# Attention and a capped mixture of experts on one core: where the gate's logits stand among the attention units, how fast the routing list is worked off, and three idle products

## The chip, the core and the metric

The kernel runs on one core of a Trainium2 chip. It is a single launch, written with a hand-made order for every engine. Times are device microseconds of one execution, as the median of several; a difference is given as time after over time before.

The engines are named as in the profile: PE is TensorE's matmul side and PEld its loading of weights (the stationary operand), which overlaps PE; DVE is VectorE, ACT ScalarE, POOL GpSimd, and SP the engine that issues most DMAs. "SPq" in a row is SP's sequencer.

## The reference

Two steps. Attention over 4 batches x 8 heads x 768 positions x 64, with a mask that leaves each position the first 8 positions and the 96 last ones up to itself, and a linear bias by distance. Then a mixture of experts on the 3072 tokens of width 512: each token goes to the expert with the greatest gate logit, and of an expert's tokens only the 80 with the greatest gate value are computed.

```python
scores = scale * np.matmul(q, k.transpose(0, 1, 3, 2)) + bias
scores = np.where(is_global | is_local, scores, -1e9)
a = np.exp(scores - np.max(scores, axis=-1, keepdims=True))
a = a / (np.sum(a, axis=-1, keepdims=True) + 1e-09)
x = np.matmul(a, v)                       # then to (3072, 512)

logits = x @ w_gate                       # 512 x 8
expert_idx = np.argmax(logits, axis=1)
gate_w = probs[np.arange(N), expert_idx]  # softmax of the logits
for e in range(8):
    tok_idx = np.where(expert_idx == e)[0]
    # if there are more than 80: keep those with the 80 greatest gate_w
    h = np.maximum(x[tok_idx] @ w1[e], 0.0)        # 512 -> 1024
    out[tok_idx] = gate_w[tok_idx, None] * (h @ w2[e])
```

All other rows of the output are zero.

## The kernel before

**Stages.** Constants and warming up, then the attention stage, then a search for each expert's threshold and the choice of its tokens, then the experts. All the loads of an SP queue (queries `q`, keys `kt`, values `va` and `vb`, expert weights `w`) and the stores of zeros and of x go through one queue in the order written down. Expert weights are loaded from early in the attention stage on.

**Units.** The 3072 tokens are 24 tiles of 128. A unit u is half a tile: tile t = u // 2, four of its eight heads (g = u % 2). The loop over units issues, for unit u and on PE in this order: the score products (L181) of u; inside them the transposes (L242, L250) of the probabilities of u - 2; and `weigh(u - 3)`, the products with the values (L289 for the local window, L298 for the part before it). On DVE stand four operations (L201) that add the bias and find the maximum of a unit, the sum's reciprocal (L213, L214), and half of the copies `ta` of the transposes (L265); on ACT four exponentials (L205) and the other half of the copies (L259); on POOL the scaling of the probabilities (L222).

**The buffer `pair`.** Both head groups of a tile are summed up in one PSUM buffer, `pair`. When its second half is done (in an even unit: u - 3 is odd), ACT copies it to `ut` (L312, `A.copy(out=uts[t]...)`). The next tile's first product L289 stands in the unit after, an odd one, and overwrites `pair`, so it waits for this copy. `ut` is a buffer for two tiles, so that it is full after every fourth unit.

**Logits.** For two tiles t and t + 1 together, four products L318 (one for each pair of heads; `logits1`) put the logits, 32 rows a pair, in the buffer `lps`. DVE copies them to `ls` (L322), two transposes L330 (`logits2`) bring `ls` back with a token in each partition, and DVE adds up the four parts for each tile (L359, in `collect`). In the loop before the change they stood by the unit's number modulo 4:

```python
if u % 4 == 1 and 9 <= u:
    logits2((u - 9) // 2, 2)      # ahead of weigh(u - 3)
...
if u % 4 == 0 and 8 <= u:
    logits1((u - 8) // 2, 2)      # directly ahead of weigh(u - 3)
```

**Routing.** The tiles form groups of 6, 6, 6, 4 and 2. When the last logits of a group are there, generators are put at the end of a list `routing`: softmax pieces (L500 to L511), compares of every token's value with 127 candidate thresholds (`choose`, L545), a count (six products L601 for a group of six, one a tile), and the columns of later one-hot products (`columns`, L581 to L588, on POOL). `routes(n)` at the end of a unit runs n steps of that list. Before the change n was 2, 3 in units with u % 4 = 3, and 5 from unit 41 on. The generator `rest` does the compares, then yields twice without an instruction, then counts.

**After the last unit** the order comes from the string DRAIN. Between the search and the experts ten products (L594, `busy`) with no use of their result keep PE running, then the experts begin: `prepare` splits a quarter of an expert's first weights into two rounded parts (L813 on ACT, L817 on DVE), three more idle products L953 use these parts (STAY), and `tokens(0)` transposes the gathered rows of the first expert (L835, copied at L836), which the first expert's products L843 take. The rows come by an indirect DMA from x; SP waits for the same rows before a small transfer (L947).

Of the kernel before, what the change touches and what calls it, by code (L numbers as in the profile page):

```python
# [22 lines left out]
P = 128  # L23
NB = S // P
NT = B * NB
# [13 lines left out]
QUARTERS = [(k, e, c) for k, e in LAYERS for c in range(4)]  # L39
NHI, NLO = (4, 1), 6  # L40
GROUPS = (6, 6, 6, 4, 2)
# [10 lines left out]
HELD, EVERY, AHEAD, LATE = 2, 3, 14, 2  # L52
FROM, INSIDE = 18, 14
HOLD = 20


DRAIN = (
# [4 lines left out]
ROWS = (3, 1, 3, 1, 0, 0, 0)  # L62
WAKE, FILL = 7, ((0, 2), (1, 4), (2, 4), (3, 1), (4, 1))
WARM = (0, 0, 0, 0, 0, 0, 2, 10)
STAY = (3, 0)
SPLIT = (4, 4, 4)
FAR = 1.0e6
END = object()
# [3 lines left out]
def fast_path(tc, a, out, cst, x_dram, inp):  # L72
    nc = tc.nc
    V, A, G, T = nc.vector, nc.scalar, nc.gpsimd, nc.tensor
    ident = cst["ident"]

    with ExitStack() as ctx:
# [6 lines left out]
        lps = psl.tile([P, 512], F32, name="lps")  # L84
# [56 lines left out]
        with tc.tile_pool(name="at_sb", bufs=2) as sp, ExitStack() as sctx:  # L141
# [13 lines left out]
            def begin(u):  # L155
                st[u] = [
                    sp.tile([P, 4], F32, tag="nm", bufs=3, name=f"nm{u}"), sp.tile([P, 4], F32, tag="z", bufs=3, name=f"z{u}"),
                    sp.tile([P, 4, WH], F32, tag="ts", name=f"ts{u}"), pwz[u % 3][:, :4 * WH].rearrange("p (j k) -> p j k", j=4),
                ]
# [156 lines left out]
            def logits1(t, n):  # L316
                for pr in range(NP):
                    T.matmul(  # L318
                        lps[32 * pr:32 * pr + 32, :n * P], cst["wgn"][:, pr, :], st[t, "ut"][:, pr, :n, :], start=True, stop=True,
                        skip_group_check=True)  # L320
                ls = sp.tile([P, n * P], F32, tag=f"ls{n}", name=f"ls{t}")
                (A.copy if t == NT - 2 else V.tensor_copy)(out=ls, in_=lps[:, :n * P])  # L322
                st[t, "l"] = ls

            def logits2(t, n):

                ls = st.pop((t, "l"))
                if n == 2:
                    for i in range(2):
                        T.transpose(out=part(t + i), in_=ls[:, P * i:P * i + P], identity=ident)  # L330
                else:
                    T.matmul(lgs(t), ls, cst["pick"], start=True, stop=True, skip_group_check=True)
                for i in range(n):
                    collect(t + i)

            def part(t):
                return lps[:, :P] if t % 2 else lps[:, 2 * P:3 * P]

            def lgs(t):
                if t == NT - 1:  # L340

                    if t not in st:
                        st[t] = psa.tile([P, 512], F32, tag="tp0", name="lgl")[:, :E]
                    return st[t]
                if t not in st:
                    st[t] = psa.tile([P, 512], F32, tag="tp1", name="lgk")[:, :E]
                return st[t]
# [28 lines left out]
            def routes(n):  # L376
                for _ in range(n):
                    while routing and next(routing[0], END) is END:
                        routing.pop(0)

            routing, cst["later"], cst["landed"] = [], [], []
            nu = 2 * NT
            late = late_constants(nc, a, cst)
            keys = inp.keys(3)
# [6 lines left out]
            for u in range(nu - 1):  # L391
                if u == 0:
                    for _ in cst["first"]:
                        pass
                begin(u)
                scores(u)
                if u % 4 == 1 and 9 <= u:
                    logits2((u - 9) // 2, 2)
                if 2 <= u:
                    copied(u - 2)  # L400
                if u == 1:
                    for _ in window:
                        pass
                    for z in pwz:
                        G.memset(z[:, 4 * WH:], 0.0)
                    G.memset(cst["zero"], 0.0)
                if u > 2:
                    for _ in range(3):
                        next(late, None)
                if u % 4 == 0 and 8 <= u:  # L410
                    logits1((u - 8) // 2, 2)
                if 3 <= u:
                    idle(2 if u == 3 else 0)
                    weigh(u - 3)
                if u % 2 == 0 and 3 <= u // 2 + 2 < NT:
                    inp.load_q(u // 2 + 2, hold=u < HOLD)
                    for _ in range(1 + (u == 20)):
                        next(keys, None)
                if u % 2:
                    if 2 <= u // 2 + 1 < NT:  # L420
                        inp.load_v(u // 2 + 1, hold=u < HOLD)
                    for k in ASKS[u // 2]:
                        next(dict(w=ahead, o=wipe).get(k, iter(())), None)
                routes(5 if u > 40 else 2 + (u % 4 == 3))
            u = nu - 1
            begin(u)
            scores(u)
# [39 lines left out]
        early = [hip.tile([P, DF], F32R, tag="hi", name=f"early{i}") for i in range(3)]  # L467
# [7 lines left out]
class Route:  # L475
# [52 lines left out]

    def rest(self, cn, capm):
        yield from self.choose()  # L530
        yield
        yield
        count(self.nc, cn, [self])
        if capm is not None:
            yield
            yield self.nc.vector.tensor_tensor(out=capm[:P - 1], in0=capm[:P - 1], in1=cn[:P - 1], op=ALU.subtract)
        yield from self.finish()
# [245 lines left out]
def experts(tc, out, cst, x_dram, inp, raw, weights, lps, early, hip, wipe):  # L783
    nc = tc.nc
    V, A, G, T = nc.vector, nc.scalar, nc.gpsimd, nc.tensor
# [3 lines left out]
    with tc.tile_pool(name="ffn", bufs=2) as fp, tc.tile_pool(name="hl", bufs=NLO) as hl, \  # L789
# [141 lines left out]
        fill, ready, held = iter(QUARTERS), {}, []  # L931
# [9 lines left out]
        with tc.manual_schedule(engines=ORDERED | {ET.SP}):  # L941
            targets(nc, cst)
            for e in range(E):
                gather(e)
                if e == 0:
                    prepare(1, True)
            nc.sync.dma_start(out=cst["scl"][:1], in_=xgs[0][:1, :2])  # L947
            for _ in islice(weights, NW - AHEAD - LATE):
                pass
            for n in range(2):  # L950
                prepare(n)
                for _ in range(STAY[n]):
                    T.matmul(lps[:, :480], early[0][:, :P], ready[QUARTERS[n]][1][:, :480], start=True, stop=True, skip_group_check=True)  # L953
            tokens(0)
            prepare(2)
            for e in range(E - 1):
                def amid(c):
                    if e == 1 and c == 2:
                        hidden(0)
                    if c == (4 if e else 2):  # L960
                        tokens(e + 1)

                layer1(e, amid)
                amid(4)
                if e:
                    layer2(e - 1, lambda c: c == 2 and hidden(e))
                    finish(e - 1)
            layer2(E - 2)
            finish(E - 2)
            last(E - 1)  # L970
            layer2(E - 1, lambda c: c == 1 and hidden(E - 1, (1,)))
            finish(E - 1)
# [487 lines left out]
```

## Time and profile before

| | |
|---|---|
| median of 3 runs | 259.3 us (257.15 to 259.46) |
| the profiled execution | 259.51 us, with a span of 257.7 us |
| busy in the span | PE 239.6 us (93%), PEld 169.2 (66%), DVE 213.7 (83%), ACT 208.0 (81%), POOL 107.5 (42%) |
| mean granted clock of PE | 0.977 |

The span is the time from the first to the last instruction; the rest of the measured time lies around it. Shares over the span mix stages, so the rows below are cut by stretches. A row of a window gives the stretch and its length, then each engine's busy time with its number of instructions (x), the granted clock of PE as a share of full speed, the share of time that the 16 DMA engines were busy, and what they moved. A row of the timeline gives start and duration, engine, line and operation, what it wrote from what with partitions x elements, how many instructions it stands for, and in square brackets how long the engine idled before it and who released it. All rows are of one execution. Matmuls are pipelined and their ends are modelled.

### The profile page before, as it was taken

Reading aid. Unit: us, or ns where it says so; the run is one execution under the profiler, and the core shown is the slowest. Engines: PE = TensorE matmul, PEld = TensorE weight load, DVE = VectorE, ACT = ScalarE, POOL = GpSimd, SP = SyncE. Lnnn points to the kernel's source line nnn. Section 1 sums busy time; section 2 is a strip of 40 time slices with the busy share of each in tenths; the row PEclk is TensorE's granted clock in tenths of the full one; section 3 lists DMA queues with packets and bytes.
Section 4 is the critical chain, followed back from the end, with each engine's and each line's share of the span. In section 5 each row is a group of like instructions: output and inputs, shape, how many; then the busy total and the mean of one; then the engine's idle time right before and its main releaser. Section 6 shows DMA issues by size and latency. Waiting matters only on the chain.

```text
span 257.7 us, 9711 instructions
## 1 busy us (share of the span) xinstructions
PE 239.6 (93%) x3587; PEld 169.2 (66%) x3587; DVE 213.7 (83%) x782; ACT 208.0 (81%) x584; POOL 107.5 (42%) x214
## 2 busy tenths in 40 slices
PE   7989998998899999999998798999999999999991
PEld 2567766766677777877667655666666666666660
DVE  3777778987779799898987778999999898999860
ACT  3889899998899999999886636887979898979740
POOL 7667674644445745457470638810000022221111
PEclk9999999999999999999999659999999999999998
DMA  5758999999998999988649976999999999999101
GB/s 145 235 159 218 330 287 280 282 304 300 274 301 247 287 284 316 319 251 230 216 138 311 384 265 204 347 333 401 404 410 408 407 397 398 389 405 364 51 25 36
DMA packets 49086, 73.06 MB, mean 284 GB/s; under 512 B 3688, under 2 KB 23528, under 8 KB 49032
## 3 DMA queue, kind: packets, MB, share of 16 engines
q1 hardware_dynamic: 47864, 69.74, 81.3%
q0 software_dynamic: 1024, 2.62, 3.2%
q8 instruction: 30, 0.49, 0.8%
q14 instruction: 24, 0.20, 0.3%
q10 hardware_dynamic: 144, 0.00, 0.0%
HBM read 58.46 MB, written 13.89 MB: 281 GB/s over the span
## 4 chain that ended last, share of the span: by engine, by line
PE 63%; ACT 13%; DVE 10%; DMA 4%; issue 4%; POOL 3%; SPq 0%; POOLq 0%; DVEq 0%; ACTq 0%
PE hp L843 17%; PE yp L843 17%; ACT pwz L205 9%; PE ring L181 6%; PE pair L289 5%; PE pair L298 3%; DMA kt<-in_kT_dram 3%; PE tp L242 3%; ACT ta L259 2%; DVE ts L201 2%; POOL pwz L222 2%; PE tp L898 2%; PE lps L318 1%; DMA q<-in_q_dram 1%; PE lps L330 1%
## 5 line engine op out<-in xcount | busy, mean ns | idle before, releaser
L205 ACT ACTIVATE pwz<-ts,nm 128x168 f32<-128x168 f32 (+1 forms) x192 | 81.5, 427 | 10.3 <-DVE z L213 6.0
L222 POOL TENSOR_TENSOR pwz<-pwz,z 128x672 f32<-128x672 f32 (+2 forms) x48 | 60.2, 1255 | 53.4 <-DVE z L214 35.5
L201 DVE CUSTOM_DVE_ANT_0 ts<-ring,tab 128x168 f32<-128x168 f32 (+1 forms) x192 | 53.2, 315 | 11.7 <-PE ring L181 11.0
L181 PE MATMUL ring<-kt,q 64*64 64x64 f32 (+3 forms) x1088 | 41.0, 275 | 1.0 <-DMA q<-in_q_dram 0.5
L926 POOL DMA_INDIRECT out_dram<-vb,si x8 | 10.0, 1248 | 76.3 <-ACT xt5h L836 37.9
L205 ACT ACTIVATION_READ_ACCUMULATOR pwz<-ts,nm 128x1 f32 x192 | 36.5, 190 | 0.0
L181 PEld LDWEIGHTS ring<-kt,q 64*64 64x64 f32 x1088 | 32.5, 137 | 4.7 <-issue 2.2
L289 PE MATMUL pair<-ta,va 104*64 104x128 f32 (+1 forms) x368 | 30.5, 285 | 5.1 <-ACT ut L312 3.5
L289 PEld LDWEIGHTS pair<-ta,va 104*64 104x64 f32 (+1 forms) x368 | 19.3, 136 | 14.1 <-issue 7.1
L265 DVE COPY ta<-tp 128x512 f32<-128x512 f32 (+2 forms) x46 | 28.3, 616 | 0.0
L259 ACT COPY ta<-tp 128x512 f32<-128x512 f32 (+2 forms) x47 | 23.8, 507 | 0.5 <-ACT pwz L205 0.5
L242 PE MATMUL tp<-ident,pwz 64*128 64x64 f32 x376 | 21.7, 235 | 1.4 <-POOL pwz L222 0.5
L242 PEld LDWEIGHTS tp<-ident,pwz 64*128 64x128 f32 x376 | 15.3, 138 | 9.1 <-POOL pwz L222 3.5
L817 DVE TENSOR_TENSOR w_3l<-w,w_3h 128x1024 fp32r<-128x1024 f32 x16 | 19.6, 1223 | 1.4 <-ACT w_3h L813 1.3
L817 DVE TENSOR_TENSOR w_0l<-w,w_0h 128x1024 fp32r<-128x1024 f32 x15 | 18.3, 1222 | 2.0 <-ACT w_0h L813 2.0
L298 PE MATMUL pair<-ta,vb 64*64 64x64 f32 x640 | 18.7, 231 | 0.0
L817 DVE TENSOR_TENSOR w_1l<-w,w_1h 128x1024 fp32r<-128x1024 f32 x15 | 18.3, 1220 | 0.0
L817 DVE TENSOR_TENSOR w_2l<-w,w_2h 128x1024 fp32r<-128x1024 f32 x15 | 18.3, 1218 | 0.0
L298 PEld LDWEIGHTS pair<-ta,vb 64*64 64x64 f32 x640 | 13.2, 133 | 6.8 <-issue 6.7
L813 ACT CAST w_3h<-w 128x1024 fp32r<-128x1024 f32 x16 | 16.7, 1045 | 0.3 <-PE yp L843 0.3
L813 ACT CAST w_2h<-w 128x1024 fp32r<-128x1024 f32 x15 | 15.9, 1058 | 1.2 <-PE hp L843 1.0
L201 DVE DVE_READ_ACCUMULATOR2_ANT nm<- 128x1 f32 x192 | 16.0, 83 | 0.0
(441 smaller groups left out, 525.9 us busy)
## 6 DMA issues: line engine op xcount, KB each, us to landing
w<-in_w_dram SPq DMA_DIRECT2D x64, 512.0 KB
kt<-in_kT_dram SPq DMA_DIRECT2D x23, 272.0 KB
out_dram<-zero SPq DMA_DIRECT2D x12, 512.0 KB
q<-in_q_dram SPq DMA_DIRECT2D x23, 256.0 KB
vb<-in_vb_dram SPq DMA_DIRECT2D x20, 256.0 KB
va<-in_va_dram SPq DMA_DIRECT2D x20, 208.0 KB
x_dram<-ta SPq DMA_DIRECT2D x28, 128.0 KB
x_dram<-kt SPq DMA_DIRECT2D x6, 256.0 KB
```

Source lines behind the costliest of these rows:

```text
L181: T.matmul(sc[hh][64 * i:64 * i + 64, pp, o:o + e - c], q[h, pr * P + 64 * i:pr * P + 64 * i + 64], kt[h, pr, c0 + c:c0 + e], start=True, ...
L201: V.tensor_tensor_reduce(out=ts[:, j, :w], in0=sc[hh][:, pp, :w], in1=tab, scale=-0.125, scalar=3.0e38, op0=ALU.add, op1=ALU.min, accum_ou ...
L205: A.activation(out=pw[:, j, :w], in_=ts[:, j, :w], func=AF.Exp, bias=nm[:, j:j + 1], scale=-1.0, accum_out=z[:, j:j + 1],)
L222: eng.tensor_tensor(out=p, in0=p, in1=zs.unsqueeze(2).broadcast_to(list(p.shape)), op=ALU.mult)
L242: T.transpose(out=tps[i][:, 64 * j:64 * j + 64], in_=pw[hs[i], o:o + P], identity=ident[hs[i], hs[i]])
L259: A.copy(out=ta[:, 0, :n], in_=tps[0][:, :n])
L265: (A.copy if u == nu - 2 else V.tensor_copy)(out=ta[:, 1, :n], in_=tp[:, :n])
L289: T.matmul(up[pp][64 * hh:64 * hh + 64], va[:n, 64 * h:64 * h + 64], ta[:n, :, 64 * j:64 * j + 64], start=g == 0 if t < NT - 1 else pp == ...
L298: T.matmul(up[pp][h, 64 * i:64 * i + 64], vb[k, i, 2 * g + pp, :], ta[k, i, 256 + 64 * pp:320 + 64 * pp], start=False, stop=True, skip_gro ...
L813: A.copy(out=hi, in_=src)
L817: V.tensor_tensor(out=lo, in0=src, in1=hi, op=ALU.subtract)
L843: T.matmul(ps, p, q, start=first and i == 0, stop=last and i == 2, skip_group_check=True)
```

## The change

Three things, in the code of the same functions:

1. The unit in which the two-tile logits stand. Up to tile 13, the products L318 of tiles t and t + 1 go from unit 2t + 8 to 2t + 9 and the transposes L330 from 2t + 9 to 2t + 11. From tile 14 on they stay.
2. The list of routing steps. `routes` runs 3 steps in units with u % 4 = 0 instead of u % 4 = 3 up to unit 28, 3 in every unit from 29 to 40, and 5 from unit 41 on as before. Between the compares and the count `rest` yields 2, 3, 4 and 2 times by group instead of twice.
3. The three idle products L953 ahead of `tokens(0)` are gone, with their table.

```diff
+PAUSE = (2, 3, 4, 2)
+SOON = 14
-STAY = (3, 0)
...
+            first = {2 * t + (9 if t < SOON else 8): t for t in range(0, NT - 4, 2)}
+            second = {2 * t + (11 if t < SOON else 9): t for t in range(0, NT - 4, 2)}
...
-                if u % 4 == 1 and 9 <= u:
-                    logits2((u - 9) // 2, 2)
+                if u in second:
+                    logits2(second[u], 2)
...
-                if u % 4 == 0 and 8 <= u:
-                    logits1((u - 8) // 2, 2)
+                if u in first:
+                    logits1(first[u], 2)
...
-                routes(5 if u > 40 else 2 + (u % 4 == 3))
+                routes(5 if u > 40 else 3 if u > 28 else 2 + (u % 4 == 0))
...
     def rest(self, cn, capm):
         yield from self.choose()
-        yield
-        yield
+        for _ in range(PAUSE[self.t0 // GROUPS[0]]):
+            yield
         count(self.nc, cn, [self])
...
             for n in range(2):
                 prepare(n)
-                for _ in range(STAY[n]):
-                    T.matmul(lps[:, :480], early[0][:, :P], ready[QUARTERS[n]][1][:, :480], start=True, stop=True, skip_group_check=True)
```

The lines of the attention functions are numbered higher by one after the change (L318 becomes L319), and later ones by three or four (L545 becomes L548, L601 L604, L843 L846).

The order of PE at the end of unit 9, from the last transpose of the probabilities (`tp`) to the next unit's first scores (`ring`), before:

```order
L250 MATMUL tp_7_715<-ident,pwz_201 128x64
L330 MATMUL lps<-ident,ls_675 128x128 x2
L289 MATMUL pair<-ta_648,va 64x128 x4
L298 MATMUL pair<-ta_648,vb_119 64x64 x8
L181 MATMUL ring_208<-kt_113,q_110 64x104
```

and after:

```order
L251 MATMUL tp_7_709<-ident,pwz_201 128x64
L319 MATMUL lps<-ut_375,wgn 32x256 x4
L290 MATMUL pair<-ta_648,va 64x128 x4
L299 MATMUL pair<-ta_648,vb_119 64x64 x8
L182 MATMUL ring_208<-kt_113,q_110 64x104
```

The four products from `ut` stood at the same place of unit 8, which now has none, and stand here in place of the two transposes of `ls`.

The same place of unit 11, before and after:

```order
L250 MATMUL tp_9_855<-ident,pwz_200 128x64
L289 MATMUL pair<-ta_794,va 64x128 x4
L298 MATMUL pair<-ta_794,vb_116 64x64 x8
L181 MATMUL ring_206<-kt_114,q_111 64x128
L181 MATMUL ring_207<-kt_114,q_111 64x128
```

```order
L251 MATMUL tp_9_845<-ident,pwz_200 128x64
L331 MATMUL lps<-ident,ls_741 128x128 x2
L290 MATMUL pair<-ta_784,va 64x128 x4
L299 MATMUL pair<-ta_784,vb_116 64x64 x8
L182 MATMUL ring_206<-kt_114,q_111 64x128
```

The two transposes stand here now, between the last transpose of the probabilities and the product that waits for the copy of `pair`.

DVE around the compares (`cf`) of the third group, tiles 12 to 17; before they stand at the end of unit 44, behind that unit's copy of the logits:

```order
L201 ISA nm_3011 128x1
L265 COPY ta_3034<-tp_42_3033 128x512
L322 COPY ls_3063<-lps 128x256
L545 TENSOR_TENSOR cf_3009<-sx_2302,kval_65 128x254 x3
L201 ISA ts_3083,nm_3081<-ring_206,tab 128x168
```

and after, at the end of unit 43:

```order
L202 ISA nm_2947 128x1
L266 COPY ta_2970<-tp_41_2969 128x512
L558 TENSOR_TENSOR oh<-eq_2429,m_2433 128x48
L548 TENSOR_TENSOR cf_3009<-sx_2432,kval_65 128x254 x3
L202 ISA ts_3016,nm_3014<-ring_207,tab 128x168
```

The compares moved ahead by a unit, and with them what follows in the list: the six counting products from unit 45 to 44. From unit 47 on the order of all engines is the same as before, but for L953.

## Rows read from the trace of the kernel before

**Rows 1.** The page's chain that ended last, by line, shares of the span.

```profile
PE hp L843 17%; PE yp L843 17%; ACT pwz L205 9%; PE ring L181 6%; PE pair L289 5%; PE pair L298 3%; DMA kt<-in_kT_dram 3%; PE tp L242 3%; ACT ta L259 2%; DVE ts L201 2%; POOL pwz L222 2%; PE tp L898 2%; PE lps L318 1%; DMA q<-in_q_dram 1%; PE lps L330 1%
```

**Rows 2.** Windows of four units, 8 to 23 and 32 to 35; columns as told above.

```profile
25.10:35.55 10.45, 9.96 (x265) 7.77 (x258) 8.49 (x50) 9.73 (x39) 7.58 (x21) 1.00 0.96 299
35.55:45.50 9.95, 8.98 (x222) 6.56 (x213) 8.14 (x49) 9.07 (x37) 5.40 (x20) 1.00 0.95 298
45.50:55.95 10.45, 9.79 (x236) 7.36 (x235) 9.45 (x55) 9.96 (x42) 5.88 (x11) 1.00 0.97 283
55.95:68.03 12.08, 10.77 (x264) 8.31 (x268) 9.10 (x55) 10.04 (x39) 4.92 (x7) 1.00 1.06 308
...
89.22:99.86 10.64, 10.25 (x278) 8.08 (x274) 9.33 (x53) 10.14 (x40) 5.85 (x8) 1.00 0.98 293
```

**Rows 3.** Windows of the single units 31, 32 and 33.

```profile
86.30:89.22 2.92, 2.43 (x77) 1.92 (x72) 2.35 (x14) 2.92 (x13) 2.10 (x4) 1.00 1.01 285
89.22:92.09 2.87, 2.87 (x85) 2.09 (x81) 2.19 (x12) 2.46 (x10) 2.17 (x5) 1.00 0.90 279
92.09:94.76 2.67, 2.67 (x79) 2.14 (x75) 2.60 (x17) 2.67 (x11) 1.20 (x2) 1.00 0.95 235
```

**Rows 4.** Timeline of units 31 to 33, PE and ACT around `pair` and `lps`.

```profile
87.79 0.56 ACT L312 COPY ut<-pair 128x512 f32<-128x512 f32 x1
...
88.41 0.42 PEld L289 LDWEIGHTS pair<-ta,va 104*64 104x64 f32 x8 [0.52 <-ACT ut L312]
...
90.71 0.64 PE L318 MATMUL lps<-ut,wgn 128*32 128x256 f32 x8
...
91.28 0.66 PE L289 MATMUL pair<-ta,va 104*64 104x128 f32 x8
...
93.57 0.20 PEld L330 LDWEIGHTS lps<-ident,ls 128*128 128x128 f32 x2
...
93.94 0.42 PEld L289 LDWEIGHTS pair<-ta,va 104*64 104x64 f32 x8 [0.17 <-ACT ut L312]
```

**Rows 5.** Waits in units 8 to 35: engine, line, releaser, us, times, longest.

```profile
PEld pair L289 <- ACT ut L312: 3.6, 8, 0.8
```

**Rows 6.** Timeline, the keys of unit 22: issue on SP and first use.

```profile
54.22 0.56 SPq L1364 DMA_DIRECT2D kt<-in_kT_dram  x1
...
62.15 0.86 PE L181 MATMUL ring<-kt,q 64*64 64x104 f32 x24 [0.45 <-DMA kt<-in_kT_dram]
```

**Rows 7.** Timeline, the third routing group on DVE, ACT and PE.

```profile
122.59 0.20 DVE L511 TENSOR_REDUCE sx<-ex 128x6 f32<-128x48 f32 x1 [0.53 <-ACT ex L508]
...
123.25 0.43 ACT L205 ACTIVATE pwz<-ts,nm 128x168 f32<-128x168 f32 x1 [0.70 <-DVE z L213]
...
127.65 0.46 PE L601 MATMUL lps<-oh,cf 128*127 128x8 bf16 x6 [0.52 <-DVE lg L359]
```

**Rows 8.** Timeline from the last idle products to the first expert.

```profile
151.60 3.18 PE L594 MATMUL lps<-svx,ones 128*128 128x480 bf16 x10
...
154.95 0.93 PE L953 MATMUL lps<-w_0l,early 128*128 128x480 f32 x3 [0.17 <-DVE w_0l L817]
...
155.60 0.77 SPq L947 DMA_DIRECT2D scl<-q  x1
155.72 0.44 PE L835 MATMUL xf<-ident,q 80*128 80x80 f32 x4
...
156.72 0.46 PE L843 MATMUL hp<-early,xt0h 128*80 128x512 f32 x1 [0.57 <-ACT xt0h L836]
```

**Rows 9.** Windows of 2 us between search and experts.

```profile
140.00:142.00 2.00, 1.22 (x27) 0.98 (x26) 1.79 (x8) 1.12 (x2) 0.00 (x0) 1.00 1.04 400
...
144.00:146.00 2.00, 1.97 (x44) 1.65 (x43) 1.64 (x7) 1.40 (x2) 1.40 (x6) 0.50 1.00 376
...
152.00:154.00 2.00, 2.00 (x7) 0.81 (x6) 1.06 (x7) 0.00 (x0) 1.50 (x3) 0.59 0.37 152
154.00:156.00 2.00, 1.83 (x11) 1.10 (x9) 2.00 (x2) 0.00 (x0) 1.74 (x1) 1.00 0.30 90
```

## The prediction

> **What bounds the kernel now.** I read the chain of work that ended last first. It gives the two expert lines L843 34% of the span and spreads the rest over the attention stage [rows 1]. The change touches only that stage (48 units) and one place between selection and experts. I then cut the attention stage into stretches of four units, from one unit's first score product to that of the fourth one after, because the change has a period of four. In each stretch TensorE and ScalarE (ACT) are both nearly full: units 8 to 11 take 10.45 us, of which PE is busy 9.96 and ACT 9.73; units 32 to 35 take 10.64, with 10.25 and 10.14 [rows 2]. So neither has much to give: 0.4 to 1.0 us in four units.
>
> Single units show how the two alternate. Unit 31 takes 2.92 us with ACT full and PE busy 2.43; unit 32 takes 2.87 with PE full and ACT busy 2.46; in unit 33 both are full for 2.67 [rows 3]. The timeline says why PE idles in unit 31: the first value product of a tile (L289, even head group) overwrites `pair`, which ACT must first have copied out (L312, begun at 87.79); the product's weights load at 88.41 after 0.52 us of idling [rows 4]. In units 8 to 35 there are eight such waits, 3.6 us together [rows 5]. I count three as some 0.2 us that can't be had: they stand behind a logits transpose, as the one of 0.17 in unit 33 does, directly after L330 [rows 4]. The other five are (3.6 - 0.6) / 5 = 0.6 us each. They lie in units 11, 15, 19, 31 and 35: odd units that follow the end of a tile and have nothing between the score transposes and L289.
>
> **The change, part by part.**
>
> *Logits and their transposes.* Four products L318 stood in the units 8, 12, ... 32, in which PE is full; from their start to L289's is 91.28 - 90.71 = 0.57 us [rows 4]. The two transposes L330 stood one unit later and cost 93.94 - 93.57 = 0.37 us [rows 4]. Now L318 stands where L330 stood and L330 two units further on, directly ahead of the waiting L289. For a group of four units the path of PE loses 0.57 (unit 4k), gains 0.57 - 0.37 = 0.20 (unit 4k+1), and in unit 4k+3 the 0.37 of L330 lies inside a wait of 0.6 where there is one. Net 0.37 saved in the groups that begin at 8, 12, 16, 28 and 32; in those at 20 and 24 there was no such wait, so L330 costs its 0.37 there and the net is nothing. Seven groups: 3 x 0.37 = 1.11 us up to unit 19, 2 x 0.37 = 0.74 us from unit 28.
>
> Not all of it arrives, for two reasons.
>
> Up to unit 19 it has to pass unit 22. There PE waits for keys: the transfer issued at 54.22 releases the score product at 62.15, 7.9 us later [rows 6], and the stretch of units 20 to 23 takes 12.08 us instead of some 10.5, with a DMA share of 1.06 [rows 2]. If the landing is fixed by full transfer engines, whatever was gained before is waited away: bound 0. If the landing moves with the issue (the queue issues as PE and the others release buffers), all 1.11 stays. The share before, 0.96, 0.95 and 0.97 in stretches of 10.45, 9.95 and 10.45 us [rows 2], leaves 0.42 + 0.50 + 0.31 = 1.2 us of transfer time unused, so an earlier issue can be served partly. I take the middle, 0.55.
>
> From unit 28 ACT sets the limit. In unit 32 it idles 2.87 - 2.46 = 0.41 us [rows 3], so of the 0.57 that leave it at most 0.41 is gained, and in unit 33, where ACT is full already, the 0.20 more of PE may be covered or not: 0.21 to 0.41 per group, against 0.37 by PE alone. I take 0.30, twice: 0.60. The same limit in the early groups, length minus ACT busy, is 0.72, 0.88 and 0.49 [rows 2] and does not bind.
>
> The Trainium skill (Perfetto Trace Analysis, Identifying the Most-Contended Engine) says that matmul busy time tells little of how near TensorE is to its limit, that its weight-load share tells more, and that for the other engines occupancy does. By that, ACT (10.14 of 10.64 in units 32 to 35) is the contended engine and not PE (weights loading 8.08), and filling PE's waits would bring nothing. The trace agrees only for the odd units.
>
> The wait that L330 gets, for DVE's copy of the logits (L322), is later by a unit than before and so no nearer. The copy (L322) and the reduction (L359) move on DVE by one and two units, and the third routing step moves from unit 4k+3 to 4k: DVE is busy 9.33 of 10.64 us in units 32 to 35 [rows 2], and the same operations are issued. Nothing.
>
> *Three steps a round, and pauses.* No instruction is added. Steps come earlier from unit 29 on, and the third group's block shifts by one unit: its three compares from unit 44 to 43, its six counting products (L601) from 45 to 44. Before, the block cost twice: a reduction on DVE waits 0.53 us for ACT's exponential and ACT then idles 0.70, and the counting products wait 0.52 for DVE's L359 and take 0.46 [rows 7]. After, the exponential stands behind a copy of `pair` on ACT (unit 42 ends a tile), so the DVE reduction waits no less; the counts stand behind the copy L322 of the same unit instead of L359. Best case: both waits go, -1.2. Worst: another 0.57 for that copy of `pair`. The like rows are the block's own, one unit earlier, so I take 0, with -0.4 to +0.5 as what I find plausible. What is queued behind the counts on PE is the next unit's scores, and DVE waits for those.
>
> *No idle products.* Three products L953 went, 0.93 us [rows 8], and they are on the chain. But L835 behind them needs the first gathered rows: the SP instruction that waits for the same gather goes at 155.60, and L835 starts at 155.72 [rows 8]. So the gather takes over as cover: gain 0 to 0.1, I take 0. What they did was keep TensorE occupied. Without them it idles from the end of the ten products of L594 at 154.8 to about 155.7, and again till 156.7 as before [rows 8].
>
> **Clock.** TensorE runs at 2.4 GHz through the attention stage; after a stretch in which it was busy 1.22 of 2 us the granted clock is 0.50 (1.2 GHz) at 144 to 146, and it is back at 1.00 at 154 to 156, after the ten products of L594 [rows 9]. The idle 0.9 us that is new is a quarter of a pause already there, and dense products follow; I take no effect. The Trainium skill (TensorE: Matmul & The Clock Gate, What's actually happening) states that throttled is the default and activity releases it, which speaks against taking idle products out; the trace shows a fall of that kind once. By that rule the first expert could run at half rate.
>
> **Sum.** 0.55 + 0.60 + 0 + 0 = 1.15 us. The profiled execution has a span of 257.7 us and a time of 259.51, within 0.3 us of the median 259.3 of the runs shown. 259.51 - 1.15 = 258.36; against the median, 258.15. I say **258.2**.
>
> **Rivals.**
>
> *All of it arrives.* The landing at unit 22 moves with its issue, PE's 1.85 us are kept, and the routing block gives 0.4: 259.3 - 2.25 = 257.05. For it: keys are issued by progress; against: ACT's full odd units.
>
> *Nothing arrives.* ACT is the bound wherever PE waits, and the transfer at unit 22 takes the rest: 259.3 us. For it: ACT is full in units 31 and 33 [rows 3]; against: 0.41 idle in unit 32.
>
> *The keys or the routing block cost.* A denser start of the stage meets a full queue and the block gets the 0.5 us: 259.8 us.
>
> *Slower: the clock stays down into the first expert.* If the low stretch, some 9 us long up to within the stretch 152 to 154, where its mean is 0.59 [rows 9], is followed by one more for want of the idle products, expert products run at half rate. Nine us at the low clock do what 4.5 us do at the high one, so +4.5 us, less the 1.15: 259.3 + 3.35 = 262.65 us. It decides from the moment the profile shows 0.50 behind 156.7 us. Against: the clock rose before L953 began, at 154.95, and not behind it.
>
> **How the numbers follow.** My forecast (a gain of 0.6 to 1.8 us, 257.5 to 258.7) has 0.47; all of it 0.22; nothing 0.16; a small cost 0.09; the clock 0.06. The range of 8 in 10 takes the forecast, most of "all" and "nothing" and half of the small cost: below, all of it with the routing block's best case, 1.2 in place of 0.4 (257.05 - 0.8 = 256.25, so 256.2); above, 259.9. Within 1% is about what a measurement of this kernel can tell from no change: 256.7 to 261.9 us. Forecast, nothing, small cost and half of "all" end there. The other half (0.11), with more from the routing block, and an eighth of the forecast (0.06), because the runs of before already spread from 257.15 to 259.46, end below. So faster 0.17, same 0.77, slower 0.06.
>
> **What would show it.** Right: L289 without a wait behind L312 in units 11 to 35; units 8, 12, ... 32 near 2.3 us instead of 2.87; a longer wait for keys at unit 22; L835 at the moment the gather lands. Wrong: unit 4k+3 as long as before with L330 in it and the wait unfilled; L601 in unit 44 waiting more than a microsecond; keys landing as much earlier as they are issued; a granted clock of 0.50 after the first expert product.

## The result and the profile after

The change made the kernel slower: 259.82 us in the median against 257.6, each of 21 runs, a ratio of 1.007 with a 95% interval of 1.005 to 1.009, so 1.8 us (1.3 to 2.3) where a gain of 1.15 was forecast. (The medians lie 2.2 us apart; the ratio leaves out one slow execution of the changed kernel, of 263.0 us.) In absolute terms 259.82 lies inside the range, but only because the first three runs of before (259.3) had come out high: its median over 21 is 257.6.

The profiled execution of the changed kernel misleads, as that of before had: its span is 257.0 us, shorter than the 257.7 of before. Executions of one kernel differ by up to 5 us, and this one (258.67) lies below its kernel's median, that of before (259.51) above. In the chain of work that ended last, ACT's exponentials and POOL's scaling have larger shares than in [rows 1], 10% and 4% against 9% and 2%:

```profile
PE yp L846 17%; PE hp L846 16%; ACT pwz L206 10%; PE ring L182 5%; PE pair L290 4%; POOL pwz L223 4%; DVE ts L202 3%; PE pair L299 3%; ACT ta L260 3%; PE tp L243 3%; DMA kt<-x_dram,gi 2%; PE lps L319 2%; PE tp L901 2%; DVE z L214 1%; ACT ut L313 1%
```

Windows of four units, 8 to 23 and 32 to 35, as [rows 2]:

```profile
24.66:34.85 10.19, 9.84 (x263) 7.57 (x259) 8.38 (x48) 9.59 (x39) 7.49 (x21) 1.00 0.89 283
34.85:44.87 10.02, 9.02 (x226) 6.61 (x218) 8.29 (x51) 9.09 (x39) 5.55 (x20) 1.00 0.98 310
44.87:55.01 10.14, 9.63 (x234) 7.36 (x235) 8.36 (x54) 9.66 (x41) 5.57 (x11) 1.00 1.00 305
55.01:65.56 10.55, 10.34 (x280) 8.08 (x275) 9.45 (x57) 10.05 (x40) 5.29 (x7) 1.00 1.01 312
86.26:96.71 10.45, 10.33 (x278) 8.07 (x274) 9.39 (x54) 10.15 (x40) 6.31 (x10) 1.00 0.99 304
```

Units 20 to 23 take 10.55 us instead of 12.08: no wait for keys. The others are within about 0.3 us of what they were. The single units 31, 32 and 33, as [rows 3]:

```profile
83.35:86.26 2.91, 2.81 (x79) 2.13 (x75) 2.34 (x16) 2.91 (x13) 2.30 (x5) 1.00 0.98 297
86.26:88.55 2.29, 2.29 (x76) 1.92 (x72) 1.87 (x11) 2.07 (x8) 1.65 (x5) 1.00 0.95 285
88.55:91.59 3.04, 2.93 (x84) 2.08 (x80) 2.60 (x17) 3.04 (x13) 2.15 (x4) 1.00 0.98 306
```

Unit 32 went from 2.87 to 2.29 us, as forecast; unit 33 from 2.67 to 3.04, not 2.87. Unit 31 has the transposes in it now, PE is busy for 2.81 us of it instead of 2.43, and it is as long as before. This holds for all such units but one: over units 8 to 35 the value products on PE waited 2.4 us for the copy of `pair` before and wait 0.3 us after.

```profile
PE pair L289 <- ACT ut L312: 2.4, 5, 0.7
```

```profile
PE pair L290 <- ACT ut L313: 0.3, 1, 0.3
```

So the waits were filled, and yet the time did not come. The same waits of the weight loads are not fewer than in [rows 5], 5.2 us in fourteen places against 3.6 in eight; seven of the fourteen, of 0.41 us, stand in the units 9, 13, ... 33 behind the four products, where PE itself is still busy with these. And the transposes (L242, then L243) wait longer for POOL's scaled probabilities, 2.1 us before and 3.8 after:

```profile
PEld tp L242 <- POOL pwz L222: 2.1, 7, 0.5
```

```profile
PEld pair L290 <- ACT ut L313: 5.2, 14, 0.6
...
PEld tp L243 <- POOL pwz L223: 3.8, 11, 0.8
```

The place that lost is the third routing group. The timeline of units 42 to 44, as [rows 7]:

```profile
116.97 0.57 ACT L313 COPY kt<-pair 128x512 f32<-128x512 f32 x1
117.43 0.24 ACT L511 ACTIVATE ex<-ex 128x48 f32<-128x48 f32 x1
...
117.71 0.20 DVE L514 TENSOR_REDUCE sx<-ex 128x6 f32<-128x48 f32 x1 [0.73 <-ACT ex L511]
...
118.25 0.43 ACT L206 ACTIVATE pwz<-ts,nm 128x168 f32<-128x168 f32 x1 [0.58 <-DVE z L214]
...
122.79 0.41 DVE L323 COPY ls<-lps 128x256 f32<-128x256 f32 x1
...
123.26 0.46 PE L604 MATMUL lps<-oh,cf 128*127 128x8 bf16 x6 [1.01 <-DVE ls L323]
...
123.75 0.16 DVE L539 TENSOR_TENSOR capm<-capm,lps 127x8 f32<-127x8 f32 x1 [0.55 <-PE lps L604]
```

The exponential (L511) now stands behind the copy of `pair`, and the sum on DVE waits 0.73 us for it (0.53 before). The counts wait 1.01 us (0.52 before), for the copy of the logits L323, since both use the same buffer `lps`; and DVE, behind them, waits 0.55 us more to subtract their result (L539). In the code the two touch different columns of `lps`, the copy 0 to 255 and the counts 384 to 391, so it is the shared buffer and not the values that puts one behind the other. That a buffer of their own would let the counts go is not shown: no run gave them one.

I measure attention from here on by DVE's first operation in each unit. From unit 42 to unit 47, before and after:

```profile
117.05:130.82 13.77, 12.74 (x320) 9.93 (x320) 12.75 (x74) 11.95 (x48) 7.49 (x11) 1.00 0.73 208
```

```profile
114.32:129.19 14.87, 12.91 (x320) 10.16 (x320) 12.62 (x71) 11.79 (x46) 6.61 (x7) 1.00 0.65 187
```

That is 1.10 us more, and it repeats: in all executions profiled in this study whose order is that of before there (five) this stretch took 13.77 or 13.78 us, and where it is that of the changed kernel (four) 14.87.

At the start of the experts, as [rows 8], the transposes L838 start at 154.26, behind SP's instruction for the same rows at 154.18:

```profile
150.21 3.90 PE L597 MATMUL lps<-svx,ones 128*128 128x480 bf16 x10
...
154.18 0.77 SPq L950 DMA_DIRECT2D scl<-q  x1
...
154.26 0.47 PE L838 MATMUL xf<-ident,q 80*128 80x80 f32 x4
...
155.31 0.46 PE L846 MATMUL hp<-early,xt0h 128*80 128x512 f32 x1 [0.57 <-ACT xt0h L839]
```

### The profile page after: what moved, and what is told of

It is laid out like the page before. It is cut to its first block, busy times and chain, and to the rows that moved or that the text cites. A ratio compares the mean times of both kernels' runs of the same rounds, so it can differ in the third digit from the quotient of the medians.

```text
span 257.0 us, 9704 instructions
## 1 busy us (share of the span) xinstructions
PE 238.5 (93%) x3584; PEld 168.2 (65%) x3584; DVE 213.7 (83%) x782; ACT 206.9 (81%) x584; POOL 106.5 (41%) x214
## 4 chain that ended last, share of the span: by engine, by line
PE 60%; ACT 15%; DVE 11%; POOL 5%; issue 4%; DMA 3%; POOLq 0%; SPq 0%; DVEq 0%; ACTq 0%
PE yp L846 17%; PE hp L846 16%; ACT pwz L206 10%; PE ring L182 5%; PE pair L290 4%; POOL pwz L223 4%; DVE ts L202 3%; PE pair L299 3%; ACT ta L260 3%; PE tp L243 3%; DMA kt<-x_dram,gi 2%; PE lps L319 2%; PE tp L901 2%; DVE z L214 1%; ACT ut L313 1%
## 5 line engine op out<-in xcount | busy, mean ns | idle before, releaser
L929 POOL DMA_INDIRECT out_dram<-vb,si x8 | 11.0, 1374 | 77.7 <-ACT va L869 42.1
L243 PE MATMUL tp<-ident,pwz 64*128 64x64 f32 x376 | 22.0, 235 | 3.2 <-POOL pwz L223 1.4
L243 PEld LDWEIGHTS tp<-ident,pwz 64*128 64x128 f32 x376 | 15.6, 138 | 11.4 <-POOL pwz L223 6.5
```

What stands on the lines that cost most here:

```text
L243: T.transpose(out=tps[i][:, 64 * j:64 * j + 64], in_=pw[hs[i], o:o + P], identity=ident[hs[i], hs[i]])
```

## The experiments

Theories at the start: the idle products' removal keeps the clock low (clock); the moved steps themselves cost (order); and the transfers take what PE gains. Ratios are to the kernel before on the same chip.

**Each part alone.** `x1_stay_back` puts the idle products back into the changed kernel, `x2_only_stay_off` takes them out of the kernel before:

```diff
                 prepare(n)
-                for _ in range(STAY[n]):
-                    T.matmul(lps[:, :480], early[0][:, :P], ready[QUARTERS[n]][1][:, :480], ...)
```

> The changed kernel with the three idle products put back ahead of the first expert; the logits and the routing steps stay as changed. Clock theory (the gap that their removal opened keeps TensorE's low clock for longer in many executions, and that alone makes the change slower): 1 to 2 us below the kernel before, some 256 us against 257.6, with a mean granted clock at or above 0.975. Order theory (the moved logits and routing steps themselves cost, as the longer wait of the counting products in unit 44 suggests): within 0.5 us of the changed kernel, 259.8 us. The two profiles show units 46 and 47 reached 1.8 us earlier after the change, which speaks for the first.

> The kernel before with nothing changed but the three idle products taken out. Clock theory: 1.5 to 3 us slower than before, about 259.5 us, and a mean granted clock lower by 0.006 to 0.012. Order theory: no difference, within 0.3 us. My prediction had costed this edit at 0.

Measured: 1.0104 (1.006 to 1.0148) and 1.000 (0.997 to 1.003). The removal costs and brings nothing, and the clock theory in this form has fallen. The cover that I had named is in the second kernel's timeline, where the products are gone: the transposes wait 0.78 us for the gathered rows.

```profile
153.31 0.48 PE L834 MATMUL xf<-ident,q 80*128 80x80 f32 x4 [0.78 <-DMA q<-x_dram,gi]
```

`x3_only_logits` and `x4_only_routing` are the kernel before with part 1 and with part 2 of the change alone, as in its diff:

```diff
+SOON = 14                     # x3
+                if u in second: ...
+                if u in first: ...
...
+PAUSE = (2, 3, 4, 2)          # x4
+                routes(5 if u > 40 else 3 if u > 28 else 2 + (u % 4 == 0))
```

> The kernel before with the logits and transposes of tiles 0 to 13 later, and nothing else. By the prediction's sum 1.15 us faster; by the profiles, where unit 40 is reached 2.7 us earlier after the change, up to 2.5 us faster. Order theory: as before or slower, 0 to +1.5 us.

> The kernel before with three routing steps a round from unit 29 and the pauses ahead of the counts, and nothing else. By the prediction 0, between -0.4 and +0.5 us. Order theory: up to 1.5 us slower, because the counting products then stand in unit 44 behind compares that are not ready (0.95 us of waiting there in the profile after).

Measured: 1.0174 (1.014 to 1.0209) and 1.0091 (1.0057 to 1.0124), so 4.5 and 2.3 us slower. The first is worse than both parts together (1.0104 in `x1_stay_back`), the second as bad. The two parts depend on each other: logits that come later push every later step of the list back, and without the new pace the counts in unit 45 come between the compares that they need. In `x4_only_routing` units 42 to 46 are short (13.63 us); there all three compares of the second group stand in one unit, and in its one profile a wait of 1.10 us for queries follows two units later. Whether that wait is what its six runs lost isn't shown:

```profile
95.34 1.17 DVE L546 TENSOR_TENSOR cf<-sx,kval 128x254 bf16<-128x254 f32 x3
...
98.86 0.86 PE L182 MATMUL ring<-kt,q 64*64 64x104 f32 x24 [1.10 <-DMA q<-in_q_dram]
```

**Is it the third group?** `y1_block_later` is the changed kernel with its steps back in units 43 to 45, `w1_counts_later` with its counts alone back in unit 45:

```diff
-                routes(5 if u > 40 else 3 if u > 28 else 2 + (u % 4 == 0))
+                routes(5 if u > 42 else 3 if u > 28 else 2 + (u % 4 == 0))   # y1
...
-PAUSE = (2, 3, 4, 2)
+PAUSE = (2, 3, 6, 2)                                                         # w1
```

> The changed kernel with one number changed: five routing steps a round from unit 43 on instead of 41, which puts the third group's exponential, compares and counts back to the units in which they stood before (43, 44, 45). Block theory (in the changed kernel the sum waits 0.73 us for an exponential that stands behind the copy of `pair` in unit 42, and the counts wait 1.01 us in unit 44; taking the shorter of two executions for each unit, units 42 to 46 together are 1.1 us longer than before): 1.1 us below the changed kernel, about 258.7 us, with unit 42 at 2.5 us instead of 3.5. Transfer theory (the loss is waiting for queries and keys in units 34 to 37): as the changed kernel, 259.8 us.

> The changed kernel with six pauses instead of four ahead of the third group's counts, which so stand at the end of unit 45 as before; the exponential and the compares stay in units 42 and 43 as changed. If the wait of the counts in unit 44 (1.01 us) is the main loss, by itself or through a lower granted clock behind it: 0.8 to 1.5 us below the changed kernel. If the exponential behind the copy of `pair` in unit 42 is (unit 42 measured 3.5 us against 2.5): at most 0.5 us below it, unit 42 still at 3.5 us, and unit 44 at 3.2 us instead of 3.6.

Measured: 0.9985 (0.9955 to 1.0015) and 1.0007 (0.9975 to 1.004), against 1.007 for the change. With its steps back, the loss is gone: it is the third group's place. Units 42 to 46 in `y1_block_later` and `w1_counts_later`:

```profile
115.43:129.62 14.19, 13.11 (x330) 10.29 (x332) 12.85 (x74) 12.32 (x50) 6.64 (x6) 1.00 0.69 211
```


```profile
115.06:129.11 14.05, 13.07 (x320) 10.12 (x320) 12.51 (x71) 11.91 (x47) 6.67 (x7) 1.00 0.72 209
```

In `y1_block_later` unit 42 is back at 2.36 us. Its five units are 0.42 us longer than those of before, but the stretch behind them is shorter by as much: from unit 42 to the first expert product it takes 39.7 us, the five executions with the order of before there 39.6 to 40.2, the four with that of the change 41.0 to 41.6, and `w1_counts_later` 40.3.

In `w1_counts_later` 0.82 of the 1.10 us went with the counts, so most of the loss is their place; the exponential and the compares, which stay a unit early there, keep the other 0.28. The measured times of the two runs are too close to settle this share; it rests on the profiles. (Unit 42 still takes 3.5 us instead of 2.5, but unit 44, which has no compares, gives back most of it.)

**Is it the transfers?** `z1_before_no_zero` and `z2_after_no_zero` leave out the two stores of zeros during attention, and with them those rows of the output:

```diff
-ASKS = "- - w w w w w w w w - o - w - o - w - - w - - -".split()
+ASKS = "- - w w w w w w w w - - - w - - - w - - w - - -".split()
...
-            for i in range(12):
+            for i in range(2, 12):
```

> The kernel before without the two stores of zeros (512 KB each) that it issues during the attention stage; their rows of the output are left unwritten. Transfer theory: 0 to 1 us faster than before, and no unit that waits for queries or keys. Block theory: as before, 257.6 us.

> The changed kernel without the same two stores of zeros (their rows are left unwritten). Transfer theory: its distance to the kernel before without them shrinks from 2.2 us to 1 us or less, about 258.2 us, and no wait for queries in units 34 to 37. Block theory: the distance stays at about 2 us, 259.6 us.

Measured: 0.9963 (0.9936 to 0.9989) and 1.0037 (1.0005 to 1.0069). The distance between the two, 0.7%, is that of the change: these stores aren't its cause.

**The early logits alone.** `y2_soon6` is `x3_only_logits` with `SOON = 6`; `w2_soon6_pause4` adds `PAUSE = (2, 2, 4, 2)`, which puts the third group's counts into unit 46.

> The kernel before with the logits and transposes of tiles 0 to 5 alone later (products in units 9, 13, 17, transposes in 11, 15, 19), and nothing else. By the prediction half of 3 x 0.37: 0.55 us faster. By the unit lengths measured since (units 8 to 19 together shorter by 0.27 us, the rest given back in the unit that has the products): 0.3 us faster or no difference. Order theory: slower, by up to 1 us, because the first group's routing steps come later.

> The kernel with only the logits of tiles 0 to 5 later (259.9 us where the kernel before had 258.2), with two more pauses ahead of the third group's counts, which so stand at the end of unit 46 with their compares done, instead of directly behind the compares in unit 45, where they waited 0.71 us and the granted clock fell to 0.50 right behind. Block and clock theory: the 1.75 us go, back to the kernel before or 0.3 us below it, mean granted clock from 0.964 to 0.973, none at 0.50 ahead of the search. If the early logits themselves cost: no change, 259.9 us.

Measured: 1.0078 (1.0046 to 1.011) and 1.0022 (0.9993 to 1.0052). Three pairs of logits changed at least sixty microseconds earlier in the program cost 2 us, and as much is lost where the list has shifted the third group: in `y2_soon6` units 42 to 46 take 15.76 us, 1.99 more than before, with PE waiting for compares in the middle of the counts, and TensorE is at its lower clock behind that:

```profile
124.51 0.22 PE L604 MATMUL lps<-oh,cf 128*127 128x8 bf16 x2 [0.20 <-DVE lg L360]
...
125.44 0.61 PE L604 MATMUL lps<-oh,cf 128*127 128x8 bf16 x4 [0.71 <-DVE cf L548]
```

```profile
124.00:126.00 2.00, 1.04 (x25) 0.84 (x21) 1.72 (x8) 1.63 (x7) 1.00 (x1) 1.00 0.04 9
126.00:128.00 2.00, 2.00 (x33) 1.61 (x32) 0.85 (x7) 0.49 (x3) 0.12 (x1) 0.52 0.63 183
114.46:130.22 15.76, 14.44 (x324) 11.29 (x326) 13.04 (x74) 12.87 (x50) 8.35 (x13) 0.89 0.64 189
```

With the counts in unit 46 the same stretch takes 13.48 us, at 1.00:

```profile
115.59:129.07 13.48, 12.82 (x324) 10.09 (x325) 12.54 (x72) 12.20 (x48) 8.33 (x13) 1.00 0.74 218
```

**Wait or clock?** `v1_soon6_fill` and `v2_fill_ahead` are `y2_soon6` with twelve idle products in the wait:

```diff
     for i, (g, t) in enumerate(todo):
+        if cst is not None and i == 2:          # v2: i == 0
+            wake = cst["svx"].rearrange("p s t -> p (s t)")
+            for _ in range(12):
+                nc.tensor.matmul(spare, wake[:, :P], wake[:, :104], start=True, stop=True, ...)
         nc.tensor.matmul(cn[:P - 1], g.cm[:, t, :], g.oh[:, t, :], ...)
```

> The kernel with only the logits of tiles 0 to 5 later (259.9 us), whose counts wait 0.71 us in unit 45, with twelve idle products of 104 columns put into that wait; the wait and everything behind it stay. Clock theory (the loss is the lower granted clock that follows the wait): most of the 1.75 us come back, 258.2 to 258.7 us, mean granted clock from 0.964 to 0.970 or more, and 1.00 through units 45 to 47. Wait theory (the wait itself is the loss): no change or slightly slower, 259.9 to 260.2 us.

> As v1_soon6_fill, but the twelve idle products of 104 columns stand ahead of the first of the six counts and not between them, so that the sums of the counts are not broken up and the kernel keeps its usual way. The compares end at the same time as before, so the counts can't begin earlier than they ended waiting; only what TensorE does meanwhile is changed. Clock theory (the loss of the kernel with early logits is the lower granted clock behind the wait, units 45 and 46 at 4.2 and 3.1 us instead of 2.7 and 2.1): 258.0 to 258.7 us instead of 259.9, and units 45 and 46 at 2.7 to 2.9 and 2.1 us. Wait theory: 259.9 us, no change.

The first took 5,859 us with 42,593 instructions instead of some 9,710: the kernel chose its general path. What the products between the accumulating counts did to these to bring that about isn't shown, and the run says nothing on the question. The second measured 1.005 (1.002 to 1.0079), between `w2_soon6_pause4` and `y2_soon6` but apart from neither by more than the intervals, so the measured times don't decide between the theories. In its profile PE is busy 1.65 of 2 us there instead of 1.04, the clock stays up, and units 42 to 46 take 14.93 us:

```profile
124.00:126.00 2.00, 1.65 (x36) 1.31 (x32) 1.99 (x11) 1.90 (x9) 1.27 (x1) 1.00 0.41 133
126.00:128.00 2.00, 1.96 (x42) 1.61 (x42) 1.00 (x9) 0.64 (x3) 0.27 (x1) 1.00 0.38 76
114.74:129.67 14.93, 14.07 (x348) 11.17 (x348) 12.93 (x74) 12.58 (x50) 8.33 (x13) 1.00 0.67 206
```

So in the one profile of each, of the 2.28 us by which 15.76 exceeds 13.48, 0.83 went with the clock and 1.45 stayed, with the wait and whatever the idle products themselves cost. By these profiles both theories were partly right. In four of the twelve executions of `v2_fill_ahead` the mean clock was 0.955 to 0.960, below all of the kernel before in the same round (0.966 and more), so the filling may not hold each time; where the clock fell in them isn't shown.

**What TensorE's time is worth.** `d1_before_double` and `d2_after_double` issue the four logits products of tiles 0 to 13 twice:

```diff
-                for pr in range(NP):
+                for pr in [*range(NP)] * (2 if t < 14 else 1):
```

> The kernel before with the four logits products of tiles 0 to 13 issued twice (the second time onto the same place; nothing else changes), so 0.57 us more of TensorE in units 8, 12, ... 32. By the prediction TensorE is the limit in these units: each of the seven gets 0.5 to 0.57 us longer and nothing is given back, 3.5 to 4 us in all. If the other engines set the pace over a group of four units, the next unit gives part of it back: 0.2 to 0.3 us for each group, 1.5 to 2 us in all.

> The changed kernel with the same products issued twice, which there stand in units 9, 13, ... 33. By the prediction these units have room (0.37 us went and 0.57 came, at a cost of at most 0.2): each gets less than 0.57 us longer, some 0.3, and 2 us in all. If TensorE's time is worth as much there as in the even units, each gets 0.57 us longer, 3.5 to 4 us in all, which is why the move gains nothing.

Measured: 1.0097 (1.0063 to 1.0131) and 1.0122 (1.0069 to 1.0175). Units 16 and 17 of four kernels show it; before, then doubled:

```profile
46.57:48.99 2.42, 2.42 (x54) 1.64 (x54) 2.16 (x14) 2.21 (x10) 1.33 (x2) 1.00 0.90 277
48.99:51.58 2.59, 2.59 (x64) 2.01 (x66) 2.40 (x16) 2.59 (x11) 1.37 (x3) 1.00 0.95 272
```

```profile
46.52:49.36 2.84, 2.84 (x62) 1.89 (x62) 2.16 (x13) 2.63 (x12) 1.34 (x2) 1.00 0.99 273
49.36:51.91 2.55, 2.55 (x64) 2.01 (x66) 2.32 (x16) 2.46 (x10) 1.37 (x3) 1.00 1.03 363
```

and the changed kernel, then doubled:

```profile
45.88:47.79 1.91, 1.88 (x44) 1.44 (x43) 1.83 (x12) 1.71 (x8) 1.08 (x1) 1.00 0.96 304
47.79:50.92 3.13, 2.85 (x70) 2.07 (x72) 2.22 (x12) 3.13 (x13) 1.62 (x5) 1.00 1.04 317
```

```profile
47.02:48.94 1.92, 1.88 (x44) 1.44 (x43) 1.83 (x13) 1.71 (x8) 1.09 (x1) 1.00 0.72 216
48.94:52.49 3.55, 3.28 (x78) 2.33 (x80) 2.22 (x13) 3.33 (x14) 1.61 (x5) 1.00 1.03 342
```

Doubling adds 0.42 us to unit 16 of the one and 0.42 to unit 17 of the other, of 0.57 put in. Over whole groups of four units, against the shortest time of the same order, it adds 0.2 to 0.5 us in the one and 0.2 to 0.7 in the other, 2.5 and 2.9 us in all seven. The measured times lie 2.5 us above the kernel before and 1.3 (some 0 to 2.8) above the change; the second, of four runs, is lower than its profile says. So by the profiles TensorE's time is worth about the same in both places, and moving the four products from one to the other can gain little.

**The low clock of the search.** `v3_before_warm` keeps TensorE running there: `WARM = (3, 1, 2, 1, 0, 2, 2, 10)` instead of `(0, 0, 0, 0, 0, 0, 2, 10)`.

> The kernel before with nine idle products of 480 columns put into waits of the search (3, 1, 2, 1, 0, 2 at the places that had none), and nothing else. If the low clock of some 10 us during the search (143.4 to 153.6 in the profile of before) can be held off this way, its products are done in half the time: up to 4 us faster, mean granted clock above 0.985. If the clock falls anyway, the nine products at 0.2 to 0.4 us each lie on the path in part: 0.5 to 2 us slower.

Measured: 1.0013 (0.9984 to 1.0041). From the first product of the search to the first of the experts, with the clock mostly up and, in `x2_only_stay_off`, down as usual:

```profile
137.46:154.01 16.55, 14.28 (x170) 8.97 (x170) 11.78 (x37) 7.24 (x10) 8.03 (x30) 0.90 0.79 288
```

```profile
138.07:154.35 16.28, 13.08 (x158) 8.69 (x159) 11.83 (x37) 7.20 (x10) 8.49 (x30) 0.69 0.81 288
```

A clock of 0.90 instead of 0.69 and no shorter: PE is not what this stage waits for, or the idle products cost what they gain. No kernel of this study that writes its whole output was shown to be faster than the kernel before.

## Why the prediction was wrong, step by step

**The logits' place.** Unit 4k lost what I said: 0.56 us in unit 8, 0.51 in unit 16, 0.58 in unit 32; 0.3 to 0.4 in units 12, 20 and 24, while unit 28 grew by 0.3. The transposes in unit 4k + 3 were as good as free in the early groups, as I said: units 11, 15 and 19 are within 0.1 us of the shortest seen with the order of before. The step that was mis-sized is unit 4k + 1: +0.20 by PE's work, measured +0.54 in unit 17 and +0.37 in unit 33. There the products came and the two transposes left, and the leaving gave nothing back. PE arrives earlier, and the transposes of the probabilities wait for POOL's scaling, which waits, through DVE's reciprocal, for ACT's exponentials. In unit 9 it is 0.33 us:

```profile
27.87 0.33 PEld L243 LDWEIGHTS tp<-ident,pwz 64*128 64x128 f32 x8 [0.33 <-POOL pwz L223]
```

Over units 8 to 35 such waits grew from 2.1 to the 3.8 us shown above. I had applied ACT's limit from unit 28 only and left it out of the early groups because the sum of a group had room; the room lies in other units than the work. Units 8 to 41 together took 88.7 to 92.0 us in four executions with the order of before there, and 88.7 to 90.7 in four with that of the changed kernel; what spreads them is waits for loads. The shortest time of each group of four units leaves most of these out, and in each group two or more of the four executions agree on it to 0.04 us:

| units | order of before | order of the change | difference | forecast, PE alone |
|---|---|---|---|---|
| 8 to 19 | 30.54 | 30.34 | -0.20 | -1.11 |
| 20 to 27 | 20.97 | 20.52 | -0.45 | 0 |
| 28 to 35 | 20.91 | 21.60 | +0.69 | -0.74 |
| 36 to 41 | 16.21 | 16.22 | 0 | 0 |

So the gain of 1.15 us did not arrive at all, and most of the early part was missing by unit 19 already, ahead of the keys of unit 22. In units 28 to 35 the new pace of the routing steps, which I had put at nothing, takes more than the logits give: `x3_only_logits`, with the logits moved and the old pace, takes 10.25 and 10.48 us in these two groups in its one profile, before 10.24 and 10.67, and the change 10.71 and 10.89. Which of the steps costs this isn't shown. `y1_block_later`, which has all of the change but the third group's place, allows a gain of up to 1.2 us and a loss of up to 0.4. The Trainium skill (Perfetto Trace Analysis, Identifying the Most-Contended Engine), which I had weighed against the trace, judges how near TensorE is to its limit by its weight loads and the arithmetic it does and not by matmul busy time. By that the filling of PE's waits brings nothing. The waits went from 2.4 to 0.3 us and nothing came, so the trace agrees in this, but not that TensorE's time is free: 0.57 us more of it cost 0.42.

**The keys of unit 22.** I read a wait of one execution [rows 6] as a limit of the kernel and took half of the early gain away with it. The wait was an accident: 10.55 us for units 20 to 23 in the changed kernel, and 10.55 in `x2_only_stay_off`, whose attention is that of before. It is also 1.7 of the 1.9 us by which the first profiled execution lay above the median.

**The routing block.** This is the step that turned the missing gain into a loss: "Best case: both waits go, -1.2. Worst: another 0.57 for that copy of `pair`. ... so I take 0". The row said 0.52 us of waiting for L359; I took the like rows for the block a unit earlier, though in that unit the buffer `lps` holds fresh logits and the counts, which write to it, must wait for the copy on DVE: 1.01 us. I had named the copy and not asked when it ends: at 123.2, behind four bias operations and the three compares moved into the unit before. The measured cost is 1.10 us, outside my -0.4 to +0.5; a wait of L601 in unit 44 of more than a microsecond was among my signs of being wrong, and it came (1.01). The rival "the routing block costs" had the mechanism, with a chance of 0.09 and 0.5 us as its price.

**The idle products.** Right: nothing, by the cover that I named.

**The clock.** The rival's place was wrong and its mechanism exists: the removal of the idle products didn't do it, but behind a wait of PE near the end of attention the granted clock is 0.50 (1.2 GHz) in the profiles of three variants: `x3_only_logits`, `y2_soon6`, and `d1_before_double`, where PE was busy 0.52 of 2 us ahead of it. The Trainium skill (TensorE: Matmul & The Clock Gate, What's actually happening) says that throttled is the default and that activity releases it; the rows of `y2_soon6` and `v2_fill_ahead` agree (1.04 and 1.65 us busy of 2, and 0.52 and 1.00 behind). In the changed kernel's own profile the clock didn't fall there.

**What stays open.** The change costs 1.8 us (1.3 to 2.3). Units 8 to 41 explain none of it by their shortest times, units 42 to 46 explain 1.10; the stretch from unit 47 to the first expert product, 26.1 to 26.7 us in four executions against 25.8 to 26.4 in five, may add 0.3. The rest, some 0.4 us within an uncertainty of 0.5, isn't shown anywhere; waits for loads that come more often after the change would be one candidate, and no run counts them.

## What to carry to other kernels

A step that is moved must be followed to the buffer that it writes: who has to have read it by then, and where that reader stands in its engine's order. Where steps run off one list, moving the first of them moves all that follow, far behind the place that was edited; look there first. And a wait for a transfer that one profile shows is worth a second execution before a term of the sum rests on it. A wait that is filled is no time gained as long as the engines behind it keep the pace: here PE's waits went from 2.4 to 0.3 us for nothing.

## What was not expected of the hardware

The same instructions take the same time from execution to execution to 0.01 us over 13.8 us (units 42 to 46, nine executions in two groups), while units 8 to 41, which wait for loads, spread over 3 us in the same profiles. By these profiles much of the spread in the measured times comes from there. And a higher clock need not bring time: 16.55 us of search at a mean of 0.90, with the idle products that held it up, against 16.28 at 0.69.
